# Taking the first four overflow tiles as one batch inside the last segment, and starting the next part's first pass later

## The chip, the cores and the metric

The kernel runs on one NeuronCore of a Trainium2 chip. The metric is the device time of one execution in microseconds (us). Before the change three runs gave 8543.35, 8543.91 and 8546.97 us, so the median is 8543.91 us. One further execution was profiled; its own time was 8539.33 us, and its trace spans 8537.6 us from the first to the last instruction.

Engines are called by their short names: PE (matrix products), DVE (vector), ACT (activation), POOL (GpSimd, which here issues every gather and scatter) and SP (which issues the plain transfers).

## The reference

640,000 edges connect 10,000 nodes. Every edge takes the 64 x 4 features of its source node, mixes the four components with a tensor that depends on the edge, scales the 64 channels with a learned radial weight, and adds the outcome to its destination node. A 64 x 64 product ends it.

```python
R = silu(edge_feat @ w_rad)                    # (E, 64)
xs = x[src]                                    # (E, 64, 4)
tp = einsum('eci,ef,ifo->eco', xs, Y, cg)      # (E, 64, 4)
agg = segment_sum((R[:, :, None] * tp).reshape(-1, 256), dst, N)
out = einsum('ncm,cd->ndm', agg.reshape(N, 64, 4), w_mix)
```

## The kernel before

**Sorting in two passes.** The edges are sorted by destination so that the sums can be matrix products. They are cut into three parts (30, 35.5 and 34.5 per cent; `SPLIT`). Pass 1 (`pass1`) routes the edges of one part into 18 groups of 576 nodes; pass 2 (`pass2`) routes the edges of one group into 18 buckets of 32 nodes. One group of one part is a *segment*. A pass first makes tables for some chunks (`digits`, `tables`: a chain of small steps that goes back and forth between PE, ACT and DVE), and then moves chunks of 12 tiles of 128 edges (`route`): DVE builds a spread payload X (line 578) and part of a one-hot matrix (594), ACT the rest of it (600, 601), PE multiplies them (608, 610), ACT evicts (615), and POOL scatters the rows to DRAM (619). In pass 2 a chunk continues the last row of the chunk before it, so PE needs the evicted chunk before (610).

**Messages.** `messages` takes the sorted buckets in units of 5 or 6 tiles: POOL gathers the source rows with one instruction per tile (line 915), DVE scales them (967), PE sums them over the edges of a bucket (980), DVE or ACT evicts the sums (1009, 1011), and in the last part PE mixes four buckets (1028), ACT evicts (1036) and SP writes the output rows (1037). The gather is five units ahead in the written order, and has seven buffers.

**Order of work.** `run` has three stages. First, pass 1 of part 0 alone. Then `groups`, in which PE, DVE and ACT keep the written order (a manual schedule) while SP and POOL are ordered by the framework. `groups` writes down one quarter step of a unit after another (`v`); before each it advances pass 1 of the next part until its share of the steps is done (`done < n * (v + 1 - at) / (end - at)`), and pass 2 of the next segment until it is paid off. At its beginning no bucket is ready yet: a loop runs pass 2 of the first segment (the small group of 7 buckets) until its payload is loaded, and takes one step of pass 1 of part 1 with each of its steps:

```python
while segs[0] not in self.pay:
    next(sort)
    if later:
        said = next(later[0][0])
        done += 0.0 if said == "held" else said or 1
```

**Overflow.** Rows of a group or a bucket that is full go to a list behind the table (`ovf`; counts in `kov`). The third stage handles these lists after everything else: `overflow_consts` builds two constants; `overflow` runs a hardware loop over the tiles of 128 rows of the first pass's list, and again over those of the second; `whole` redoes all edges if a table could not hold a case (a loop over zero or one). Each loop turn (`add`, line 1206) loads one tile, gathers its source rows (1210), finds rows with the same destination (1215 to 1228), reads the present output rows with a gather (1231), forms the messages (1246 to 1251), sums duplicates and mixes (1255, 1261), adds (1263) and scatters the rows back (1264). The loops' counts are read into registers (1154, 1181).

Of the kernel before, what the change touches and what calls it, by code (L numbers as in the profile page):

```python
# [40 lines left out]
FAR = 2097152.0  # L41
KR = 108
# [31 lines left out]
class Kernel:  # L74
    def __init__(self, ctx, tc, x, src, dst, Y, ef, w_rad, cg, w_mix, out):
# [45 lines left out]
        for q, tiles in ((self.p1, [z - a for a, z in self.part]), (self.p2, sum(self.gt, []))):  # L121
            q.none = -(-(q.ovf + sum((t + q.T - 1) // q.T for t in tiles) * P + 16) // q.stride) * q.stride
            q.rows = q.none
# [20 lines left out]
    def consts(self):  # L144
# [8 lines left out]
        self.zr = c.tile([16, max(self.p1.rw, self.p2.rw)], F, name="zr")  # L153
        nc.vector.memset(self.zr, 0.0)
        self.pid = iota("pid", [[0, 1]], cm=1)
        self.pid1 = iota("pid1", [[0, 1]], base=1, cm=1)
# [905 lines left out]
    def groups(self):  # L1062
# [12 lines left out]
        later, at = [], 0  # L1075
# [6 lines left out]
        while segs[0] not in self.pay:  # L1082
            next(sort)
            if later:
                said = next(later[0][0])
                done += 0.0 if said == "held" else said or 1
        acc = 0.0
        i = start = 0
        for v in range(4 * u):
# [13 lines left out]
            if i + 1 < len(segs):  # L1103
# [20 lines left out]
    def overflow_consts(self):  # L1124
        nc = self.nc

        m = self.ph.tile([P, 4], F, name="io", bufs=1)
        nc.gpsimd.iota(m, pattern=[[-1, 4]], base=P, channel_multiplier=1, allow_small_or_imprecise_dtypes=True)
        mi = self.ph.tile([P, 4], I32, name="ioi", bufs=1)
        nc.vector.tensor_copy(mi, m)  # L1130
        nc.vector.tensor_scalar(mi, mi, 3, None, op0=OP.bitwise_and)
        nc.vector.tensor_scalar(m, mi, 0.0, None, op0=OP.is_equal)
        self.wx = self.ph.tile([P, 2, 64, 4], F, name="wx")
        for h in range(2):
            nc.vector.tensor_tensor(self.wx[:, h], self.wm2[:, h, :].unsqueeze(2).to_broadcast([P, 64, 4]),
                                    m.unsqueeze(1).to_broadcast([P, 64, 4]), op=OP.mult)

        self.L = self.ph.tile([P, P], F, name="L")
        nc.vector.tensor_scalar(self.L, self.i128, self.pid, None, op0=OP.is_lt)

    def overflow(self, ps, count):

        nc, tc, wk, pm_ = self.nc, self.tc, self.ph, self.ps

        cp = pm_.tile([P, 512], F, name="cp", tag="misc", bufs=1)
        nc.tensor.matmul(cp[:16, 0:1], self.ones[0:1, :16], count, start=True, stop=True)
        zi = wk.tile([P, 1], I32, name="zi")
        nc.vector.scalar_tensor_tensor(zi[:16], cp[:16, 0:1], float(ps.ovf), self.pid[:16], op0=OP.add, op1=OP.add)
        nc.gpsimd.indirect_dma_start(
            out=ps.dst, out_offset=bass.IndirectOffsetOnAxis(ap=zi[:16, :], axis=0), in_=self.zr[:, :ps.rw],  # L1150
            in_offset=None, bounds_check=ps.rows - 1, oob_is_err=False)
        ni = wk.tile([1, 1], I32, name="ni")
        nc.vector.tensor_scalar(ni, count, ps.r / 128.0, 127.5 / 128 - 0.5, op0=OP.mult, op1=OP.add)
        n = nc.values_load(ni, min_val=0, max_val=(ps.rows - ps.ovf) * ps.r // P)
        flat = ps.dst.rearrange("r w -> (r w)")

        def load(k):
            pay = wk.tile([P, W], F, name="opay")
            nc.sync.dma_start(pay, flat[bass.ds(k * (P * W) + ps.ovf * ps.rw, P * W)].rearrange("(s w) -> s w", w=W))
            si = wk.tile([P, 1], I32, name="osi")  # L1160
            nc.vector.tensor_scalar(si, pay[:, 0:1].bitcast(I32), (1 << 14) - 1, None, op0=OP.bitwise_and)  # L1161

            dk = wk.tile([P, 1], I32, name="odk")
            nc.vector.tensor_scalar(dk, pay[:, 0:1].bitcast(I32), 14, None, op0=OP.logical_shift_right)  # L1164
            dst = wk.tile([P, 1], F, name="odst")
            nc.vector.tensor_scalar(dst, dk, 1.0 - TD, None, op0=OP.add)  # L1166
            return pay, si, dst

        with tc.For_i(0, n, 1) as k:  # L1169
            self.add(*load(k))  # L1170

    def whole(self):

        nc, wk = self.nc, self.ph
        m = wk.tile([64, 1], F, name="om")
        nc.vector.tensor_scalar(m, self.most, P + 0.5, None, op0=OP.is_ge)
        cp = self.ps.tile([P, 512], F, name="cw", tag="misc", bufs=1)
        nc.tensor.matmul(cp[0:1, 0:1], self.ones[:64, 0:1], m, start=True, stop=True)  # L1178
        ni = wk.tile([1, 1], I32, name="nw")
        nc.vector.tensor_scalar(ni, cp[0:1, 0:1], 1.0, None, op0=OP.min)  # L1180
        n = nc.values_load(ni, min_val=0, max_val=1)
        assert self.N % 125 == 0
# [3 lines left out]
        def load(k):  # L1186
            pay = wk.tile([P, W], F, name="opay")
            nc.vector.memset(pay, 0.0)
            si = wk.tile([P, 1], I32, name="osi")
            dk = wk.tile([P, 1], I32, name="odk")  # L1190
            t = bass.ds(k, 1)
            nc.sync.dma_start(si, self.src[:, t])
            nc.sync.dma_start(dk, self.dst[:, t])
            nc.sync.dma_start(pay[:, 1:5], self.Y[:, t, :].rearrange("p t f -> p (t f)"))
            nc.sync.dma_start(pay[:, 5:9], self.ef[:, t, :].rearrange("p t f -> p (t f)"))
            dst = wk.tile([P, 1], F, name="odst")
# [3 lines left out]
        with self.tc.For_i(0, n, 1):  # L1200
            nc.sync.dma_start(self.out.rearrange("(p b) f -> p b f", p=125),
                              zo.unsqueeze(1).to_broadcast([125, self.N // 125, 256]))
            with self.tc.For_i(0, self.NT, 1) as k:
                self.add(*load(k))

    def add(self, pay, si, dst):

        nc, wk, pm_ = self.nc, self.ph, self.ps
        xg = wk.tile([P, 64, 4], F, name="oxg")
        nc.gpsimd.indirect_dma_start(  # L1210
            out=xg.rearrange("p c i -> p (c i)"), out_offset=None, in_=self.x,
            in_offset=bass.IndirectOffsetOnAxis(ap=si, axis=0))

        pd = pm_.tile([P, 512], F, name="opd", tag="misc", bufs=1)
        nc.tensor.matmul(pd[:, :P], dst.to_broadcast([P, P]), self.ident, start=True, stop=True)
        eq = wk.tile([P, P], F, name="oeq")
        nc.vector.tensor_scalar(eq, pd[:, :P], dst, None, op0=OP.is_equal)

        dup = wk.tile([P, P], F, name="odup")
        nc.vector.tensor_tensor(dup, eq, self.L, op=OP.mult)  # L1220
        skip = wk.tile([P, 1], F, name="oskip")
        nc.vector.tensor_reduce(skip, dup, axis=AX.X, op=OP.max)
        em = wk.tile([P, 1], F, name="oem")
        nc.vector.tensor_scalar(em, dst, 0.5, None, op0=OP.is_lt)
        nc.vector.tensor_tensor(skip, skip, em, op=OP.max)
        di = wk.tile([P, 1], I32, name="odi")
        nc.vector.scalar_tensor_tensor(skip, skip, FAR, dst, op0=OP.mult, op1=OP.add)
        nc.vector.tensor_scalar(di, skip, -1.0, None, op0=OP.add)
        cur = wk.tile([P, 256], F, name="ocur")
        nc.vector.memset(cur, 0.0)  # L1230
        nc.gpsimd.indirect_dma_start(
            out=cur, out_offset=None, in_=self.out, in_offset=bass.IndirectOffsetOnAxis(ap=di, axis=0),
            bounds_check=self.N - 1, oob_is_err=False)

        pT = pm_.tile([P, 512], F, name="opT", tag="misc", bufs=1)
        nc.tensor.transpose(pT[:W, :P], pay, self.ident)
        sT = wk.tile([W, P], F, name="osT")
        nc.scalar.activation(sT, pT[:W, :P], AF.Copy)
        pr = pm_.tile([P, 512], F, name="opr", tag="misc", bufs=1)
        nc.tensor.matmul(pr[:, :80], sT, self.wo, start=True, stop=True)  # L1240
        R = wk.tile([P, 64], F, name="oR")
        nc.scalar.activation(R, pr[:, :64], AF.Silu)
        A = wk.tile([P, 16], F, name="oA")
        nc.scalar.activation(A, pr[:, 64:80], AF.Copy)
        V = wk.tile([P, 64, 4], F, name="oV")
        nc.vector.tensor_tensor(V, xg, R.unsqueeze(2).to_broadcast([P, 64, 4]), op=OP.mult)  # L1246
        M = wk.tile([P, 64, 4], F, name="oM")
        for o in range(4):
            nc.vector.tensor_scalar(M[:, :, o], V[:, :, 0], A[:, o:o + 1], None, op0=OP.mult)  # L1249
            for i in range(1, 4):  # L1250
# [83 lines left out]
```

## Time and profile before

| stage of the profiled execution | from, us | to, us |
|---|---|---|
| pass 1 of part 0, alone | 0 | about 512 |
| pass 2 of the first segment, with pass 1 of part 1 | 514.2 | 614.0 (first gather of a unit) |
| units, with pass 1 of the next part and pass 2 | 614.0 | 8466.8 (last plain output write has landed) |
| overflow lists: three tiles, all of the second pass | 8466.8 | 8537.6 |
| span / own time of this execution | | 8537.6 / 8539.33 |
| median of the three runs | | 8543.91 |

A row of the timeline gives the start, the duration, the engine, the line, the operation with its tiles and shapes, the count, and in brackets how long the engine had been idle and what ended that. A row of the windows gives, for a stretch, its length, each engine's busy time with the number of instructions, the granted TensorE clock (1.00 is full speed), the share of the DMA engines and their rate. A row of the grouped lines gives a line's count, its busy time and mean, and the idle time of the engine before it with what ended it.

### The profile page before, as it was taken

The numbers are of one execution on the slowest core, as the hardware profiler recorded it, in microseconds if no ns is written. First come the engines' busy times: TensorE is split into PE (matmuls) and PEld (weight loads), VectorE is DVE, ScalarE is ACT, GpSimd is POOL, SyncE is SP. The second block draws the span as 40 slices with busy tenths as digits, with TensorE's granted clock in tenths as the row PEclk, the third lists the DMA queues.
The fourth block names the chain that finished last, engine by engine and source line by source line (L and its number), as shares of the span: only waits on it lengthen the run. The fifth ranks groups of instructions, "written<-read, shape, count | busy, mean of one in ns | idle before, by whom it ended". The sixth has DMA issues, their size and how long they took to land. (4 is left out here: it accounts for less than half of the span.)

```text
span 8537.6 us, 148817 instructions
## 1 busy us (share of the span) xinstructions
PE 6849.6 (80%) x51885; PEld 6294.3 (74%) x51885; DVE 6833.0 (80%) x12901; ACT 4467.9 (52%) x12655; POOL 5984.1 (70%) x6255
## 2 busy tenths in 40 slices
PE   7977888888888788787787888876888878787875
PEld 6867777777778677777777777766777777677764
DVE  8988898889898789888888988876767767676743
ACT  6866666666566465555555655533433434343421
POOL 2236777677677767777777777777777777777774
PEclk9989999999899899899998998988888988898887
DMA  8313444344334434444444444444444444444442
GB/s 177 101 58 98 121 118 125 108 122 118 113 116 124 124 112 138 130 135 136 132 135 136 134 135 134 131 140 130 130 125 128 127 126 127 125 126 124 127 124 80
DMA packets 694591, 1056.58 MB, mean 124 GB/s; under 512 B 250979, under 2 KB 498340, under 8 KB 693840
## 3 DMA queue, kind: packets, MB, share of 16 engines
q0 software_dynamic: 284864, 746.68, 30.0%
q1 hardware_dynamic: 406384, 292.76, 12.3%
q8 instruction: 410, 6.72, 0.3%
q10 hardware_dynamic: 2592, 7.63, 0.3%
q14 instruction: 341, 2.79, 0.1%
HBM read 856.08 MB, written 203.45 MB: 124 GB/s over the span
## 5 line engine op out<-in xcount | busy, mean ns | idle before, releaser
L915 POOL DMA_INDIRECT xg<-in_x_dram,sidx x5321 | 5062.2, 951 | 1709.2 <-issue 1386.7
L608 PE MATMUL pr<-X,oh 128*128 128x135 f32 (+1 forms) x21112 | 2783.1, 291 | 400.2 <-ACT rt L615 256.8
L608 PEld LDWEIGHTS pr<-X,oh 128*128 128x128 f32 x21112 | 2662.8, 203 | 481.3 <-ACT rt L615 315.1
L980 PE MATMUL G<-S,xg 128*128 128x128 f32 x21284 | 2872.2, 296 | 155.5 <-DVE Gp L1009 116.7
L980 PEld LDWEIGHTS G<-S,xg 128*128 128x128 f32 x21284 | 2723.8, 210 | 198.7 <-DVE Gp L1009 142.9
L967 DVE TENSOR_TENSOR xg<-xg,pre 128x1536 f32<-128x1536 f32 (+1 forms) x939 | 1559.0, 1660 | 918.0 <-DMA xg<-in_x_dram,sidx 701.7
L600 ACT ACTIVATE sq<-i,rowf 128x128 f32<-128x128 f32 x6106 | 1876.1, 392 | 5.6 <-DVE rowf L565 2.4
L578 DVE TENSOR_TENSOR X<-dv,Wt 128x1512 f32<-128x1512 f32 (+3 forms) x905 | 1579.7, 1746 | 147.0 <-PE pr L608 100.0
L949 ACT ACTIVATE pre<-pre 128x384 f32<-128x384 f32 (+1 forms) x939 | 430.4, 458 | 1391.4 <-PE pre L946 1099.4
L601 ACT ACTIVATE oh<-sq,ones 128x896 f32<-128x896 f32 (+2 forms) x905 | 964.3, 1066 | 28.8 <-issue 1.4
L960 DVE TENSOR_TENSOR S<-dv,pay 128x768 f32<-128x768 f32 (+1 forms) x939 | 857.5, 913 | 64.3 <-PE G L980 20.1
L619 POOL DMA_INDIRECT grp<-rt,idx x417 | 418.6, 1004 | 573.8 <-ACT rt L615 244.9
L594 DVE TENSOR_TENSOR oh<-dv,rowf 128x640 f32<-128x640 f32 (+2 forms) x870 | 719.3, 831 | 0.5
L933 PE MATMUL pre<-identb,e 128*108 128x128 bf16 x1878 | 273.7, 229 | 500.6 <-DVE xg L967 492.9
L933 PEld LDWEIGHTS <-e 128*108 128x108 bf16 x1878 | 219.7, 132 | 572.1 <-issue 505.8
L619 POOL DMA_INDIRECT bkt<-rt,idx x488 | 488.6, 1001 | 192.5 <-issue 111.2
L938 ACT ACTIVATE sT<-pre 108x256 bf16<-108x256 f32 x939 | 351.5, 374 | 424.6 <-PE pre L933 423.2
L1028 PE MATMUL po<-wf,Gs 128*128 128x256 f32 (+2 forms) x1392 | 401.4, 453 | 160.0 <-DVE Gs L1009 158.8
L1028 PEld LDWEIGHTS po<-wf,Gs 128*128 128x128 f32 (+2 forms) x1392 | 289.8, 214 | 251.2 <-DVE Gs L1009 164.6
L896 ACT ACTIVATE e<-er 128x360 bf16<-128x360 f32 (+3 forms) x420 | 188.9, 450 | 416.1 <-DVE er L906 415.5
L615 ACT ACTIVATE rt<-pr 128x135 f32<-128x135 f32 (+1 forms) x905 | 242.5, 272 | 286.3 <-DMA bkt<-rt,idx 213.9
L548 ACT ACTIVATE pc<-pp 128x432 f32<-128x432 f32 (+4 forms) x453 | 233.5, 515 | 254.2 <-DVE pos L557 131.9
(247 smaller groups left out, 5257.3 us busy)
## 6 DMA issues: line engine op xcount, KB each, us to landing
xg<-in_x_dram,sidx POOLq DMA_INDIRECT x5321
sums<-Gp SPq DMA_DIRECT2D x626, 128.0 KB
old<-sums SPq DMA_DIRECT2D x626, 128.0 KB
bkt<-z SPq DMA_DIRECT2D x24, 994.5 KB
pay<-bkt SPq DMA_DIRECT2D x34, 486.0 KB
ys<-in_Y_dram SPq DMA_DIRECT2D x104, 96.0 KB
es<-in_edge_feat_dram SPq DMA_DIRECT2D x104, 96.0 KB
out_dram<-ot SPq DMA_DIRECT2D x69, 128.0 KB
```

What stands on the lines that cost most here:

```text
L578: nc.vector.tensor_tensor(X[:, :m, :].rearrange("p t (s w) -> p t s w", w=W), msk.unsqueeze(3).to_broadcast([P, m, ps.r, W]), QD[c // Q][1 ...
L594: nc.vector.tensor_tensor(oh[:, :v, :], self.v128.unsqueeze(1).to_broadcast([P, v, P]), row[:, o:o + v].unsqueeze(2).to_broadcast([P, v, P ...
L600: nc.scalar.activation(sq[:, u, :], self.i128, AF.Square, bias=to, scale=-1.0)
L601: nc.scalar.activation(oh[:, v:v + len(at), :], sq[:, :len(at), :], AF.Relu, bias=self.ones[:, 0:1], scale=-2.0)
L608: nc.tensor.matmul(pr[:, :ps.rw], oh[:, u, :], X[:, u, :], start=(u == 0), stop=(not on and u == m - 1))
L619: st = nc.gpsimd.indirect_dma_start(out=ps.dst, out_offset=bass.IndirectOffsetOnAxis(ap=idx[:, i:i + 1], axis=0), in_=RT.pop(c), in_offset ...
L915: nc.gpsimd.indirect_dma_start(out=xg[:, t, :], out_offset=None, in_=self.x, in_offset=bass.IndirectOffsetOnAxis(ap=si[:, u:u + 1], axis=0))
L933: nc.tensor.matmul(pre[:KR, 256 + 128 * h:384 + 128 * h], e[:, 36 * t:36 * t + KR], self.identb, start=True, stop=True)
L960: nc.vector.tensor_tensor(S[:, :ut], self.eq[:, :ut].unsqueeze(3).to_broadcast([P, ut, NB, 4]), pb[:, :, 1:5].unsqueeze(2).to_broadcast([P ...
L967: nc.vector.tensor_tensor(V, V, R.unsqueeze(3).to_broadcast([P, ut, 64, 4]), op=OP.mult)
L980: nc.tensor.matmul(G[:, h].rearrange("p n f -> p (n f)"), V[:, t, 32 * h:32 * h + 32, :].rearrange("p c i -> p (c i)"), S[:, t].rearrange( ...
L1028: nc.tensor.matmul(po[:nn, :256], Gs[:, h, f].rearrange("p b n -> p (b n)")[:, :nn], self.wf[:, h, f, :], start=(h + f == 0), stop=(h + f ...
```

## The change

Three things change.

1. The first four tiles (`LT = 4`) of the second pass's overflow list are handled in `batch`, whose steps are written between the quarter steps of the last segment, once that segment is sorted. It loads the four tiles with one transfer, gathers their source rows with four POOL instructions, compares all 512 destinations with each tile, and forms, sums and mixes the messages, with buffers that the sort no longer needs. Its reading and writing of the output rows (`put`) is written after the last unit. So that the four tiles can be read whatever their count is, `clear_buckets` zeroes the list's first 35 rows at the beginning.
2. What is left (the first pass's list, tiles beyond the fourth, `whole`) is put into one hardware loop over zero or one (`rest`), whose count `remains` has worked out in the last segment. Inside it, the loops take four tiles a turn.
3. The loop at the beginning of `groups` no longer takes steps of pass 1, and pass 1 of part 1 starts at quarter step 40 instead of 0.

```diff
-        later, at = [], 0
+        later, at = [], 40
...
         while segs[0] not in self.pay:
             next(sort)
-            if later:
-                said = next(later[0][0])
-                done += 0.0 if said == "held" else said or 1
+        batch, got = self.batch(), None
...
+            elif got is None:
+                if segs[-1] in self.pay:
+                    run(sort)
+                    self.remains()
+                    got = "begun"
+            elif got != "ready":
+                got = next(batch) or got
             next(main)
         assert not later
-        run(main)
-        run(sort)
+        for _ in main:
+            if got != "ready":
+                got = next(batch) or got
+        while got != "ready":
+            got = next(batch) or got
+        run(batch)
...
+    def clear_buckets(self):
+        a, m = self.p2.ovf, -(-LT * P // self.p2.r)
+        nc.sync.dma_start(self.p2.dst[a:a + m, :], self.z[:m, :self.p2.rw])
...
+    def join(self, al, pay, dst, di, xg, wx):
+        for t in range(OT):                      # 512 destinations against each tile
+            nc.tensor.matmul(pd[:, t * P:t * P + P], dst[:, t:t + 1].to_broadcast([P, P]), self.ident, ...)
+        for t in range(OT):
+            nc.vector.tensor_scalar(eq[t // 2][:, t % 2], pd, dst[:, t:t + 1], None, op0=OP.is_equal)
...
+        nc.vector.tensor_tensor(xg, xg, R..., op=OP.mult)        # 128 x 1024
+        for i in range(4):                       # four products and three sums of 128 x 1024
...
+        for h in range(2):                       # 32 matmuls 128 x 128, then 8 of 128 x 256
...
+    def put(self, al, di, xg):
+        nc.vector.memset(cur, 0.0)
+        for t in range(OT):
+            nc.gpsimd.indirect_dma_start(out=cur[:, t], in_=self.out, in_offset=...di[:, t:t + 1]...)
+        for t in range(OT):
+            nc.vector.tensor_tensor(cur[:, t], cur[:, t], xg[:, t]..., op=OP.add)
+            nc.gpsimd.indirect_dma_start(out=self.out, out_offset=...di[:, t:t + 1]..., in_=cur[:, t])
...
+    def rest(self):
+        with self.tc.For_i(0, self.nc.values_load(self.n[:, 3:4], min_val=0, max_val=1), 1):
+            self.wide(wx)
+            self.leftover(self.p1, self.kov[:, 0:1], self.n[:, 0:1], 0, wx)
+            self.leftover(self.p2, self.kov[:, 1:2], self.n[:, 1:2], LT * P, wx)
+            self.whole(self.n[:, 2:3], wx)
...
-            self.overflow_consts()
-            self.overflow(self.p1, self.kov[:, 0:1])
-            self.overflow(self.p2, self.kov[:, 1:2])
-            self.whole()
+            self.rest()
```

More of the change, by code (lines that the diff above doesn't have):

```diff
@@ L1163, in load @@
[L1163 to L1166, printed above, removed]
-            return pay, si, dst
-        with tc.For_i(0, n, 1) as k:
-            self.add(*load(k))
-    def whole(self):
-        nc, wk = self.nc, self.ph
[L1175 to L1182, printed above, removed]
+            pay = wk.tile([P, OT, W], F, name="opay")
```

280 lines of the change are left out of this document (187 added, 93 removed).

## The prediction

> **What bounds the kernel now.** I read the grouped lines first, then POOL's idle time over the first two parts, then the timelines of the places that the change touches: the beginning of the second stage, the last segment, the end. The page, and POOL's grouped lines between 1000 and 2800 us:
>
> ```profile
> span 8537.6 us, 148817 instructions
> L915 POOL DMA_INDIRECT xg<-in_x_dram,sidx x5321 | 5062.2, 951 | 1709.2 <-issue 1386.7
> ...
> L915 POOL DMA_INDIRECT xg<-in_x_dram,sidx x1142 | 1088.7, 953 | 391.0 <-issue 289.1 <-PE G L980 32.2 <-PE pre L946 8.8
> L619 POOL DMA_INDIRECT grp<-rt,idx x129 | 129.7, 1005 | 60.7 <-issue 25.0 <-ACT rt L615 7.9 <-ACT e L896 6.9
> L619 POOL DMA_INDIRECT bkt<-rt,idx x100 | 100.1, 1001 | 30.7 <-issue 21.9 <-ACT sq L600 1.5 <-ACT Gp L1011 1.2
> ```
>
> A gather takes 0.95 us and comes 0.30 us after the one before: 1.25 us each. In those 1800 us POOL has 1371 instructions: 1318.5 us busy and 1371 x 0.30 = 411 us between them; of 482.4 us idle only 71 (4 per cent) are real waits. So POOL's instruction count paces the units, and the other engines wait for it. Two stretches lie outside that: the beginning (no gather until 614 us) and the end.
>
> ```profile
> 514.00:614.00 100.00, 61.90 (x366) 51.42 (x366) 74.06 (x240) 49.73 (x150) 7.76 (x8) 0.69 0.11 31
> 520.00:540.00 20.00, 9.43 (x46) 6.05 (x47) 17.11 (x88) 2.11 (x11) 0.00 (x0) 0.50 0.07 23
> ...
> 8448.32 0.95 POOL L915 DMA_INDIRECT xg<-in_x_dram,sidx  x1 [0.30 <-issue]
> 8466.83 0.29 DVE L1139 TENSOR_SCALAR L<-i,pid 128x128 f32<-128x128 f32 x1 [6.33 <-DMA out_dram<-ot]
> 8467.17 0.13 DVE L1153 TENSOR_SCALAR ni<-kov 1x1 int32<-1x1 f32 x1
> 8472.42 0.20 PE L1146 MATMUL cp<-kov,ones 1*16 1x1 f32 x2 [7.42 <-ACTq L1154]
> 8480.13 1.03 POOL L1231 DMA_INDIRECT ocur<-out_dram,odi  x1 [1.72 <-DVE odi L1228]
> 8517.92 3.43 DMA oxg<-in_x_dram,osi
> 8530.33 1.03 POOL L1264 DMA_INDIRECT out_dram<-ocur,odi  x1 [8.68 <-DVE ocur L1263]
> 8533.72 0.19 PE L1178 MATMUL cw<-om,ones 64*1 64x1 f32 x2 [4.13 <-issue]
> 8533.94 0.14 DVE L1180 TENSOR_SCALAR nw<-cw 1x1 int32<-1x1 f32 x1 [3.90 <-PE cw L1178]
> ```
>
> The last plain output write has landed at 8466.8; all behind it, 8537.6 - 8466.8 = 70.8 us, is the overflow stage, a serial chain with everything else idle. Its list holds three tiles (the loop turned three times, for the second pass's list only), so `batch` takes all of them.
>
> **The end, part by part.** Removed: the 70.8 us. Added in the last segment: POOL's four gathers, 4 x 1.25 = 5.0 us, paid in full since POOL paces that segment; its queue has no wait there, and the indices are ready long before POOL, which lags the written order, comes to them. Also added there is the batch's work on PE, DVE and ACT:
>
> ```profile
> 8200.00:8270.00 70.00, 47.99 (x317) 43.52 (x316) 31.30 (x42) 11.07 (x28) 52.94 (x57) 0.85 0.49 140
> ...
> L967 DVE TENSOR_TENSOR xg<-xg,pre 128x1536 f32<-128x1536 f32 x9 | 15.8, 1755 | 36.2 <-DMA xg<-in_x_dram,sidx 36.2
> ...
> L980 PE MATMUL G<-S,xg 128*128 128x128 f32 x240 | 33.8, 305 | 0.6 <-DVE Gs L1009 0.5
> ...
> 8484.86 1.19 PE L1255 MATMUL opm<-oeq,oM 128*128 128x128 f32 x4 [4.71 <-DVE oM L1251]
> ```
>
> A PE row counts two records for one product of 128 columns. DVE: eight operations over 1024 columns at 1755 x 1024 / 1536 = 1.17 us are 9.4, some 8 for the comparisons and the small ones: 17 us, where DVE idles 70 - 31.3 = 38.7, nearly all of it (36.2) waiting for gathers. PE: 32 summing products, 12 short ones, 8 of double width, as 60 products: at the segment's 33.8 / 120 = 0.28 us 17 us, at the idle stage's 1.19 / 2 = 0.60 us 36 us, where PE idles 22. The steps take some 30 quarter steps, 7.5 units. POOL has seven buffers and may run about four units (30 us) ahead while PE is late, and some 20 units are left to catch up. So I cost it at nothing; without that cover it is at most 36 - 22 = 14 us. The batch's load stands in SP's queue behind fetches of old sums, and DVE's decoding of it is in the written order: behind it wait the products of one unit, 7.5 us at most, under the same cover. `remains` (some nine operations of 0.14 us and one product) is hidden likewise.
>
> Behind the last unit `put` stays. From the landing: four gathers of output rows at 1.03 + 0.30 = 1.3 us; the fourth starts 3.9 us on and lands 3.43 us later, at 7.3. Then four scatters. One takes 8533.72 - 8530.33 = 3.4 us until the next work can go on. Whether the four wait for one another the trace can't show: the loop ends between them. Chained they end at 7.3 + 13.6 = 20.9; unchained at 7.3 + 3.9 + 3.4 = 14.6. I take the chain: all four write one tensor, and `put` lacks the declaration of independence that the stores of line 619 have (lines 622 to 624). The jump over `rest`: nearest rows are the end of before (8537.6 - 8533.94 = 3.7) and the entry of the first, empty loop (8472.42 - 8467.17 = 5.2); nothing if it passes under the last scatter. I take 3.7. Sum: 70.8 - 20.9 - 3.7 - 5.0 = 41.2 us saved; between 70.8 - 20.9 - 5.2 - 5.0 = 39.7 and 70.8 - 14.6 - 5.0 = 51.2.
>
> The trace's one scatter decides 3.4 us a link. The Trainium skill, "DMA: Bandwidth & Descriptors" (section "Two DMAs through the same engine are not ordered"), says that only a completion semaphore orders dependent transfers, which speaks for the chain; its section "Anatomy of one DMA — SWDGE (gpsimd) path" gives about 2.0 us plus bytes / 436e3, for 131 KB an estimate of 2.3 us a link, with which the chain would be 9.2 and not 13.6 us. The measurement decides.
>
> **The beginning.** In the 100 us before the first gather the sort of the first segment (four chunks) shares the written order with pass 1 of part 1:
>
> ```profile
> 517.68 0.20 DVE L782 TENSOR_SCALAR dg<-Wt 128x40 int32<-128x40 int32 x1 [3.15 <-DMA Wt<-grp]
> 537.09 0.16 DVE L514 TENSOR_TENSOR idx<-rk,dest 128x4 int32<-128x4 f32 x1
> 546.47 1.84 DVE L578 TENSOR_TENSOR X<-dv,Wt 128x1620 f32<-128x1620 f32 x1
> 559.74 1.85 DVE L578 TENSOR_TENSOR X<-dv,Wt 128x1620 f32<-128x1620 f32 x1 [3.48 <-PE pr L608]
> ...
> 562.82 0.34 DVE L575 TENSOR_TENSOR dv<-dv,slot 128x168 f32<-128x168 f32 x1
> 563.28 1.73 DVE L578 TENSOR_TENSOR X<-dv,Wt 128x1512 f32<-128x1512 f32 x1
> ...
> 587.68 4.40 PE L608 MATMUL pr<-X,oh 128*128 128x126 f32 x24 [4.65 <-ACT rt L615]
> 592.12 0.72 DVE L578 TENSOR_TENSOR X<-dv,Wt 128x540 f32<-128x540 f32 x1 [0.35 <-PE pr L608]
> 592.49 2.95 PE L608 MATMUL pr<-X,oh 128*128 128x135 f32 x24
> 597.13 0.81 DVE L594 TENSOR_TENSOR oh<-dv,rowf 128x640 f32<-128x640 f32 x1
> 604.69 0.97 POOL L619 DMA_INDIRECT bkt<-rt,idx  x1 [2.47 <-ACT rt L615]
> 606.84 0.38 SPq L822 DMA_DIRECT2D pay<-bkt  x1
> 614.04 0.99 POOL L915 DMA_INDIRECT xg<-in_x_dram,sidx  x1 [8.38 <-DVE didx L869]
> ...
> L619 POOL DMA_INDIRECT grp<-rt,idx x4 | 3.9, 970 | 71.0 <-ACT rt L615 71.0
> ```
>
> The tables take 19.6 us (517.7 to 537.3), the way to the first X 9.2, four chunks a pitch of about 15 us (559.74 to 592.12 are two), the last X to the last store 12.6, store to payload load 2.2, load to first gather 7.2. Without pass 1 I take 16.5 for the tables (their steps stay serial), 6 to the first X, a pitch of 5 (PE's 4.40 at the low clock plus the carried row), 8 to the last store, and 5 more for the tables of the next segment, which run beside: 517.7 + 16.5 + 6 + 15 + 8 + 5 + 2.2 + 7.2 = 577.6. The first gather comes 36 us earlier. Bounds: nothing, if the chain only waits; 45 by the work, since pass 1's share of DVE's 74.06 us is about eight chunks of 0.34 + 1.73 + 0.81 + 0.3 = 3.2 (26 us) and one table chain (15), 41 in all, and waits go with it.
>
> The clock is 0.50 between 520 and 540 us and a chunk's 24 records take 4.40 us at one place and 2.95 at another. This agrees with the Trainium skill, "TensorE: Matmul & The Clock Gate" (section "HAM oscillation — how this bites in real kernels"), which warns of idle gaps of PE over about 3.4 us; it speaks against the change, as pass 1's products filled gaps. By full clock the ramp would be about 4 us shorter than I sum.
>
> What is moved must still be done: eight chunks and a table chain go into the units between quarter step 40 and the end of part 0. On POOL these are only the four stores that ran before 614 us, 4 x 1.27 = 5.1 us; the other engines' 41 us are hidden if POOL's pace hides them, and given back in full if not. POOL waits 4 per cent, so I take a value near the lower end, 15 us. The moved transfers of SP (destinations, sources, payload of the first blocks) stand behind writes of sums there, and DVE's decoding of them waits in the written order, once, inside these 15. Net gain 36 - 15 = 21 us; between 45 - 5 = 40 gained and 41 lost, if the ramp isn't shortened and all comes back.
>
> The constants moved to the start and the zeroing of 35 rows cost some 0.5 us.
>
> **Sum.** 41.2 + 21 - 0.5 = 61.7 us. The profiled execution's 8539.33 (1.7 above its span) becomes 8477.6; that execution was 4.6 us faster than the median of the runs shown, so against the median it is 8543.9 - 61.7 = 8482 us. 0.2 per cent, 17 us, is about what a measurement can tell from no change.
>
> **Rivals.**
> *The beginning gives nothing* (0.2): the 36 us come back from the other engines. For: DVE is busy three quarters of that stretch and more later. Against: POOL's 4 per cent. 8543.9 - 41.2 + 0.5 = 8503.
> *All bounds well* (0.12): scatters unchained, jump hidden, 40 at the beginning. 8543.9 - 51.2 - 40 = 8453.
> *The written order, not POOL, sets part 0* (0.04, slower): the table chain of pass 1, some 20 hand-offs between PE, ACT and DVE, now stops running units, at about 2 us each (40), with its 41 us of work, and the ramp is not shorter. It decides once this costs more than the end saves: 81 - 41 = 40 slower, 8584. Against: it needs 80 us more of POOL waits where 1800 us have 71.
> *The change does not do what it says* (0.04): the loops of `rest` still turn, through a fourth list or a fifth tile. Three entries of 5.2 us and one turn of about 25 undo the end's gain: 8523. Against: three tiles.
>
> The forecast has 0.6. The range reaches from the best case to the first rival with the last segment's cover gone (8503 + 14), rounded outwards: 8450 to 8518. It leaves out the last two. Faster by over 0.2 per cent: 0.6 + 0.2 + 0.12 = 0.92 (the last rival lies about on the line); within 0.04; slower 0.04.
>
> **What would show it.** Right: no loop turns behind the last plain write; four gathers 1.3 us apart, four scatters 3.4 us apart (1.3 if unchained), end some 25 us after the landing; four more POOL gathers in the last segment with no wait beyond 0.30; first unit gather near 578 us; POOL waits between 600 and 2800 us up by no more than about 15. Wrong: a first gather after 600, POOL waiting for PE in the last segment, or POOL's waits in part 0 up by 40.

## The result and the profile after

The changed kernel takes 8498.58 us in the median of six runs (8493.23 to 8501.77); the kernel before, on the same chip, takes 8546.07 us (8543.35 to 8549.97). The ratio is 0.9944, 95% interval 0.9931 to 0.9956: 47.5 us less. The prediction said 8482 us, so it forecast 61.7 us and got 47.5. The profiled execution of the changed kernel took 8493.53 us. In this document, "the lead" at the n-th gather (counted from 0) is how much earlier that gather of source rows for the units starts than in the kernel it is compared with.

First the span and the POOL rows between 1000 and 2800 us of the changed kernel (the line numbers have moved: 915 is now 926, 619 is 630, 980 is 991).

```profile
span 8491.8 us, 148473 instructions
...
L926 POOL DMA_INDIRECT xg<-in_x_dram,sidx x1120 | 1067.4, 953 | 406.4 <-issue 294.8 <-PE G L991 59.7 <-PE pre L957 10.1
L630 POOL DMA_INDIRECT grp<-rt,idx x129 | 129.5, 1004 | 62.9 <-issue 25.9 <-ACT rt L626 12.6 <-DVE rk L523 5.3
L630 POOL DMA_INDIRECT bkt<-rt,idx x100 | 100.3, 1003 | 34.1 <-issue 21.0 <-ACT rt L626 3.7 <-DVE dv L968 2.1
```

The gather still takes 0.95 us. Counted as in the prediction, POOL's real waits in these 1800 us are the idle 503.4 us less 1349 x 0.30, that is 98.7; they were 71. And there are 1120 gathers where there were 1142: the units run slower here.

The beginning, from the timeline of the changed kernel:

```profile
541.85 1.84 DVE L589 TENSOR_TENSOR X<-dv,Wt 128x1620 f32<-128x1620 f32 x1
...
545.47 1.84 DVE L589 TENSOR_TENSOR X<-dv,Wt 128x1620 f32<-128x1620 f32 x1
...
561.48 0.97 POOL L630 DMA_INDIRECT bkt<-rt,idx  x1 [0.80 <-ACT rt L626]
...
572.22 0.99 POOL L926 DMA_INDIRECT xg<-in_x_dram,sidx  x1 [9.77 <-DVE didx L880]
```

The first X stands at 541.9 us, the second 3.6 us behind it, the last store at 561.5, and the first unit gather at 572.2 where it was at 614.0.

The end, from the timeline of all engines:

```profile
8434.45 0.94 POOL L926 DMA_INDIRECT xg<-in_x_dram,sidx  x1 [0.30 <-issue]
...
8458.17 1.01 POOL L1242 DMA_INDIRECT ocur<-out_dram,osm  x1 [22.78 <-issue]
8459.49 1.00 POOL L1242 DMA_INDIRECT ocur<-out_dram,osm  x1 [0.31 <-issue]
...
8460.79 1.18 POOL L1242 DMA_INDIRECT ocur<-out_dram,osm  x1 [0.30 <-DMA ocur<-out_dram,osm]
...
8462.27 0.99 POOL L1242 DMA_INDIRECT ocur<-out_dram,osm  x1 [0.30 <-issue]
...
8465.80 1.03 POOL L1247 DMA_INDIRECT out_dram<-ocur,osm  x1 [2.53 <-DVEq L1378]
8469.35 1.00 POOL L1247 DMA_INDIRECT out_dram<-ocur,osm  x1 [2.53 <-issue]
8472.26 0.97 POOL L1247 DMA_INDIRECT out_dram<-ocur,osm  x1 [1.91 <-issue]
8475.23 0.97 POOL L1247 DMA_INDIRECT out_dram<-ocur,osm  x1 [1.99 <-issue]
```

No loop turns. Four gathers of output rows stand 1.3 to 1.5 us apart, four scatters 2.9 to 3.6 us apart. But the span ends at 8491.8, 16.6 us after the last scatter has started. What lies there are instructions of POOL's sequencer, which the timeline doesn't show; the instructions by line do (line, engine, instruction, count: duration in ns least/median/most, first and last start). In the changed kernel, the loop's line 1378 and the line of the program's end:

```profile
L1378 POOLq INC_SWDGE_SEM  x1: 1979/1979/1979, 8477.8 to 8477.8; - x1
...
L1444 POOLq DRAIN  x3: 40/103/7417, 8483.5 to 8491.5; - x3
```

And in the kernel before, the line of its first loop:

```profile
L1169 POOLq DRAIN  x4: 41/1269/7864, 8489.4 to 8515.3; - x4
L1169 POOLq INC_SWDGE_SEM  x3: 226/253/1786, 8469.0 to 8515.0; - x3
```

The last transfer is in at 8477.8; then POOL works 2.0 us on a semaphore step (INC_SWDGE_SEM) and, from 8483.5 on, 7.4 us on a DRAIN. The kernel before had the same pair, but around its first loop turn: the step of 1.8 us at 8469.0, ahead of that turn, and the DRAIN of 7.9 us at 8489.4, just behind its scatter. Later ones there took 0.23 to 0.25 us and 0.04 to 2.5 us.

The account of the two profiled executions, which differ by 45.8 us in span:

| stretch | before, us | after, us | difference |
|---|---|---|---|
| start to the first unit gather | 614.0 | 572.2 | -41.8 |
| first unit gather to the 5100th | 7553.7 | 7573.5 | +19.8 |
| 5100th to the last (the batch's place) | 280.6 | 288.8 | +8.2 |
| last unit gather to the first work behind the last plain write | 18.5 | 23.7 | +5.2 |
| from there to the end | 70.8 | 33.6 | -37.2 |

(In the kernel before the first work behind the last plain write is the row of 8466.83; in the changed one it is the gather of 8458.17.)

### The profile page after: what moved, and what is told of

It reads as the page before. It is cut to its first block, busy times and chain, and to the rows that moved or that the text cites. A ratio compares the mean times of both kernels' runs of the same rounds, so it can differ in the third digit from the quotient of the medians.

```text
span 8491.8 us, 148473 instructions
## 1 busy us (share of the span) xinstructions
PE 6828.0 (80%) x51942; PEld 6287.4 (74%) x51942; DVE 6828.5 (80%) x12848; ACT 4463.2 (53%) x12650; POOL 5986.1 (70%) x6256
## 5 line engine op out<-in xcount | busy, mean ns | idle before, releaser
L619 PE MATMUL pr<-X,oh 128*128 128x126 f32 (+1 forms) x21112 | 2775.1, 291 | 398.8 <-ACT rt L626 233.7
L612 ACT ACTIVATE oh<-sq,ones 128x896 f32<-128x896 f32 (+2 forms) x905 | 964.1, 1065 | 28.5 <-ACT sq L611 0.9
L971 DVE TENSOR_TENSOR S<-dv,pay 128x768 f32<-128x768 f32 (+1 forms) x939 | 857.5, 913 | 64.6 <-PE G L991 20.9
L605 DVE TENSOR_TENSOR oh<-dv,rowf 128x640 f32<-128x640 f32 (+1 forms) x870 | 720.1, 831 | 0.5
```

Source lines behind the costliest of these rows:

```text
L605: nc.vector.tensor_tensor(oh[:, :v, :], self.v128.unsqueeze(1).to_broadcast([P, v, P]), row[:, o:o + v].unsqueeze(2).to_broadcast([P, v, P ...
L612: nc.scalar.activation(oh[:, v:v + len(at), :], sq[:, :len(at), :], AF.Relu, bias=self.ones[:, 0:1], scale=-2.0)
L619: nc.tensor.matmul(pr[:, :ps.rw], oh[:, u, :], X[:, u, :], start=(u == 0), stop=(not on and u == m - 1))
L971: nc.vector.tensor_tensor(S[:, :ut], self.eq[:, :ut].unsqueeze(3).to_broadcast([P, ut, NB, 4]), pb[:, :, 1:5].unsqueeze(2).to_broadcast([P ...
```

## The experiments

In the session of the first four experiments every kernel, the one before included, took about 10.6 ms; their ratios are to the kernel before in that session, and the two that this concerns were run again later.

**The end alone, and the beginning alone.** For the end alone:

```diff
-        later, at = [], 40
+        later, at = [], 0
...
         while segs[0] not in self.pay:
             next(sort)
+            if later:
+                said = next(later[0][0])
+                done += 0.0 if said == "held" else said or 1
```

> The end of the change alone: the batch beside the last segment and the one loop behind it, with pass 1 of part 1 begun at the start as in the kernel before. Theory (the sizes read from the traces): the end's stage is 36 us shorter, four more gathers cost 5 us, so about 30 us faster than before (8516 us), the first unit gather near 614 us, the stage behind the last plain output write about 34.5 us. Rival 1 (the sum of the prediction holds for the end, and the beginning gives less than half of what was forecast): 41 us faster (8505 us). Rival 2 (the beginning gives nothing at all): 47 us faster (8499 us).

Measured: 10559.41 against 10591.88 us, ratio 0.9975 (0.9965 to 0.9985), 32 us less by the medians and 26 by the ratio, near the theory's 30.

The beginning alone makes the opposite edit to the kernel before (at = 40, no pass 1 in the loop).

> The beginning alone: the kernel before with pass 1 of part 1 begun at quarter step 40 of the units, its end untouched. Theory: the first unit gather is some 42 us earlier (near 572 us), some 23 us come back between the first and the last gather, net 18 us faster (8528 us). Rival 1 (the forecast's 15 us given back): 27 us faster (8519 us). Rival 2 (the beginning gives nothing, the work that is moved comes back in full): no change, 8546 us, the first gather earlier and the last one at the old place.

Measured: 10586.65 us, ratio 0.9999 (0.9988 to 1.0009). There the beginning gave nothing, as in rival 2. The POOL row of that run says why it is another case:

```profile
L915 POOL DMA_INDIRECT xg<-in_x_dram,sidx x5321 | 5071.9, 953 | 3270.4 <-issue 1413.2 <-PE G L980 828.4 <-remote 558.7
```

POOL's gathers have 3270 us of idle time ahead of them, 1857 of it real waits (1709 and 322 in the first profile): in that session POOL did not pace the units. The 20th gather had a lead of 47.0 us on the kernel with the end alone, the 80th 75.6, the 400th 28.5, the 1400th none: it was 9.6 us late. With POOL waiting for other engines, the moved work came back in full. Why that session was slower is not settled: the granted TensorE clock was 0.83 in it and 0.90 in the others, and its stage of units had waits on every engine that the kernel before doesn't show elsewhere. Both kernels were run again later, where the kernel before took 8553.4 us.

> The end alone, on a chip where the gathers pace the units again. Theory (from the times of the n-th gather in the kernels before and after): the end's stage gives 36 us, the last segment takes 8 us back (four gathers at 1.25 and 3 us more), so 28 us faster than before less what the last plain write happens to cost: 8516 to 8521 us; the n-th gather within 3 us of the kernel before up to the 5100th. Rival: the whole 47.5 us are the end's, 8499 us.

Measured: 8525.68 us, ratio 0.9969 (0.9957 to 0.9981), 27.7 us less.

> The beginning alone, on a chip where the gathers pace the units again. Theory: the 80th gather is 70 us earlier than before, 46 us of it come back by the 1400th, and 22 us stay to the end: 8524 us. Rival 1: all of it comes back, as on the chip where every kernel took 10.6 ms: 8546 us. Rival 2: the 15 us that the prediction gave back, with the 70 us that are really won: 8491 us.

Measured: 8532.49 us, ratio 0.9974 (0.9965 to 0.9983), 20.9 us less. 27.7 + 20.9 = 48.6, and the whole change gave 47.5: within the intervals, about 10 us each way, the two halves add up. The theory's split holds: about 28 us from the end, about 21 from the beginning.

**Where pass 1 begins.** Two kernels change only the start of pass 1 in the units:

```diff
-        later, at = [], 40
+        later, at = [], 0        # at0; 400 in at400
```

> The changed kernel with pass 1 of part 1 beginning at quarter step 0 of the units (not 40), still none of it beside the first sort. Theory (moved work costs the same wherever it stands in part 0, about two thirds of what it had cost at the beginning): the first gather stays at 572 us, the 80th is only some 45 to 50 us earlier than in the kernel before, the lead at the 1400th is 22 us as with 40; 8498 us, within 4 us. Rival (the units' first 40 quarter steps without pass 1 are what gives the 22 us): the lead falls to 0 to 10 us, 8508 to 8520 us.

> The changed kernel with pass 1 of part 1 beginning at quarter step 400, so that it is done in 728 quarter steps and not in 1088, half again as dense. Theory (the moved work is paid wherever it stands): the lead at the 400th gather is 100 us or more and falls to 15 to 25 us by the 1400th, 8498 us within 6 us. Rival 1 (GpSimd paces, and hides the work until a bound): the dense stretch passes that bound, the lead at the 1400th is negative, 8525 us or more. Rival 2 (the stretch without pass 1 hides more than the dense one costs): 8480 us.

Measured, in the session of the second runs: 8494.40 us with 0, ratio 0.9935 (0.9919 to 0.9950); 8597.54 us with 400, ratio 1.0052 (1.0036 to 1.0067). By the ratios the start at 0 can't be told from the changed kernel's 0.9944, and 8494.40 even lies in the 8498 within 4 us that its theory gave; the gathers tell more. The start of the n-th unit gather in the four kernels of that session, from their timelines (us; the first column has pass 1 as in the kernel before, the others give their lead on it, and the last row is the difference of two starts over 800):

| n | the end alone | the beginning alone (40) | at0 | at400 |
|---|---|---|---|---|
| 0 | 626.7 | 43.7 | 49.7 | 46.1 |
| 80 | 789.6 | 67.1 | 51.9 | 71.8 |
| 400 | 1283.9 | 50.0 | 41.0 | 125.1 |
| 600 | 1608.4 | 48.4 | 39.1 | 141.1 |
| 1400 | 2859.1 | 19.1 | 35.8 | -71.3 |
| 5100 | 8176.8 | 13.6 | 33.6 | -75.1 |
| us a gather, 600 to 1400 | 1.563 | 1.600 | 1.568 | 1.829 |

The theory of both expectations falls: the moved work isn't paid alike wherever it stands (at the 1400th gather the lead of at0 is 35.8 us where the theory said 22), and at400 ended 44 us slower than the kernel before, as its rival 1 said. The table shows a loan. Units without pass 1 beside them run at (1158.8 - 717.8) / 320 = 1.378 us a gather in at400 (80th to 400th), so a later start gains while it lasts. But pass 1 has to be done by quarter step 1128: from 0 it has 1128 quarter steps, from 40 it has 1088 (4 per cent denser), from 400 it has 728 (55 per cent denser). With 0 the units keep the old pace, 1.568 against 1.563. With 40 they lose 0.037 us a gather, 30 us in 800 gathers, and more than the loan of the first 40 quarter steps (67.1 - 51.9 = 15 us) is gone; with 400 they lose 0.266.

POOL's grouped rows between 1600 and 2850 us, in the changed kernel, with 0 and with 400:

```profile
L926 POOL DMA_INDIRECT xg<-in_x_dram,sidx x783 | 745.9, 953 | 280.9 <-issue 207.4 <-PE G L991 33.2 <-PE pre L957 8.5
L630 POOL DMA_INDIRECT grp<-rt,idx x87 | 87.4, 1004 | 40.2 <-issue 18.6 <-DVE rk L523 5.3 <-DVE oh L605 4.9
```

```profile
L926 POOL DMA_INDIRECT xg<-in_x_dram,sidx x800 | 762.3, 953 | 272.7 <-issue 207.5 <-PE G L991 22.6 <-PE pre L944 5.3
L630 POOL DMA_INDIRECT grp<-rt,idx x85 | 85.3, 1004 | 37.1 <-issue 15.8 <-ACT rt L626 7.5 <-ACT e L907 6.1
```

```profile
L926 POOL DMA_INDIRECT xg<-in_x_dram,sidx x678 | 647.1, 954 | 331.4 <-issue 169.9 <-PE G L991 98.8 <-PE stp L468 21.3
L630 POOL DMA_INDIRECT grp<-rt,idx x120 | 120.7, 1006 | 75.5 <-ACT rt L626 39.3 <-issue 19.5 <-DVE oh L605 4.5
```

Gathers per 1250 us fall from 800 to 783 to 678. More stores of pass 1 explain part of it (85, 87, 120 of them, 1.3 us each), waits for PE's products (PE G) more: 22.6, 33.2 and 98.8 us. So the cover of POOL's pace has no room left at the density of the kernel before, which is what the prediction's "POOL waits 4 per cent" hid. Which of the other engines sets that limit the rows don't settle: with 400, in the same 1250 us, DVE is busy 1106 us and PE 1053.

**The drain at the end.** One line, ahead of the batch's gathers of output rows, behind the last unit's gathers:

```diff
         while got != "ready":
             got = next(batch) or got
+        self.tc.keep_in_program_order(self.nc.gpsimd.drain())
         run(batch)
```

> The changed kernel with one more GpSimd drain, between the last unit's gathers and the four gathers of output rows, where GpSimd idles for 23 us. Theory: the 7.4 us of the drain at the very end are paid once for all the gathers and stores since the last drain; taken in the idle stretch they leave under 1.5 us for the drain at the end: 6 to 7 us faster than the changed kernel (8492 us). Rival 1 (the drain's 7.4 us belong to the four scatters ahead of it, or to the end of a program): the last drain still takes about 7.4 us and the time stays at 8498 us. Rival 2 (the early drain keeps GpSimd until after the batch is ready): the four gathers start later than before, no gain or a loss of up to 4 us.

Measured: 10552.00 us, ratio 0.9969 (0.9959 to 0.9979). That alone can't be told from the 0.9975 of the end without it. The trace can: the extra drain took 14.96 us, but it begins at 10444.4, beside the last gathers of the units, which end at 10452.5; 6.8 us of it lie behind them, in a stretch in which POOL waited 41.5 us for the plain writes anyway. The one at the end took 0.71 us instead of 7.42 and the semaphore step 0.34 instead of 1.98, and from the first gather of output rows to the end of the span are 10519.1 - 10494.0 = 25.1 us, where the changed kernel has 33.6. The theory's 6 to 7 us became 8.5: 6.7 of the drain, as it said, and 1.6 of the semaphore step, which it didn't name.

Is it the first drain that is dear, or what has piled up since the last one? The same line ahead of the second stage:

```diff
+        self.tc.keep_in_program_order(self.nc.gpsimd.drain())
         while segs[0] not in self.pay:
             next(sort)
```

> The changed kernel with one more GpSimd drain just ahead of the second stage (behind some 130 of the 6240 GpSimd transfers), where GpSimd is idle for over 50 us. It tells a first-time cost from a backlog. Theory 1 (the drain pays for the transfers issued since the last one): the early drain is short or as long as its transfers take to land, the one at the end still takes 7.4 us and the semaphore step ahead of it 2.0 us; the time is that of the changed kernel. Theory 2 (what costs is the first drain of a program): the last drain takes under 1 us, the step ahead of it about 0.3 us, 8 us faster than the changed kernel.

Measured: 8501.28 us in the one run (the kernel before 8551.32). The early drain, the semaphore step and the drains at the end:

```profile
L1093 POOLq DRAIN  x1: 3353/3353/3353, 518.2 to 518.2; - x1
...
L1379 POOLq INC_SWDGE_SEM  x1: 1619/1619/1619, 8487.4 to 8487.4; - x1
...
L1445 POOLq DRAIN  x3: 46/103/5937, 8492.7 to 8499.2; - x3
```

An early drain leaves 5.9 of the 7.4 us and 1.6 of the 2.0 us at the end. So neither theory holds in full, but most of the cost is not that of a first drain; it goes with what POOL has done since the last one (about 6100 transfers here, eight in drain_idle). It doesn't go with the time: the last drain took 7.417 us in the kernel with the end alone in the session of 10.6 ms and in that of 8.5 ms. Nor is it in plain proportion to the transfers: only 123 of 6238 stand ahead of the early drain here, and a fifth of the cost is gone. How it grows between 8 and 6100 was not tried.

**Four scatters without a chain.** `put` lacks the declaration that the passes' stores have:

```diff
-            nc.gpsimd.indirect_dma_start(
+            st = nc.gpsimd.indirect_dma_start(
                 out=self.out, out_offset=bass.IndirectOffsetOnAxis(ap=di[:, t:t + 1], axis=0), in_=cur[:, t], in_offset=None,
                 bounds_check=self.N - 1, oob_is_err=False)
+            if t:
+                self.tc.declare_no_dep(st.ins, group=key, reason="the rows of a batch are apart")
+            self.tc.add_to_no_dep_group(key, st.ins)
```

> The changed kernel with the four scatters of the batch declared independent of one another, as the stores of the passes are. Theory: the four scatters were chained at 3.0 to 3.5 us a link; without the chain they follow each other by their issue of 1.3 us, 5 to 6 us faster (8493 us). Rival 1 (the transfers themselves queue behind one another): the starts are 1.3 us apart, and the last one lands no earlier, 8498 us. Rival 2: the drain at the end takes up what the chain gave, growing from 7.4 us to 12 or more.

Measured: 10553.89 us, ratio 0.9967 (0.9956 to 0.9978). From the first gather of output rows to the end 10544.7 - 10516.5 = 28.2 us instead of 33.6: 5.4 less, as the theory said. The last drain stayed at 7.42 us, so rival 2 falls, and rival 1 with it.

**Both, and then with the start at 0.**

> The changed kernel with both: the extra GpSimd drain in the idle stretch behind the last gathers, and the four scatters declared independent. Theory: the two gains lie behind one another on the chain of the end, so they add up: 8 us from the drain (with the shorter semaphore step ahead of it) and 5 to 6 us from the scatters, the stage behind the last plain output write shrinks from 34.5 to about 21 us, the whole 61 us faster than the kernel before where the changed kernel was 47.5 us faster. Rival: without the chain the last drain finds transfers still under way, and takes back 3 us or more.

Measured: 8479.17 us (8478.45 to 8482.64) against 8545.97, ratio 0.9923 (0.9909 to 0.9937), 66.8 us less. The end of it, from the timeline, and then its drains (1137 is the extra one) and its semaphore step by line:

```profile
8434.84 0.94 POOL L926 DMA_INDIRECT xg<-in_x_dram,sidx  x1 [0.30 <-issue]
8457.43 1.01 POOL L1245 DMA_INDIRECT ocur<-out_dram,osm  x1 [21.64 <-DMA out_dram<-ot]
...
8465.14 1.03 POOL L1250 DMA_INDIRECT out_dram<-ocur,osm  x1 [2.59 <-DVEq L1384]
8466.47 1.00 POOL L1250 DMA_INDIRECT out_dram<-ocur,osm  x1 [0.30 <-issue]
8467.78 0.97 POOL L1250 DMA_INDIRECT out_dram<-ocur,osm  x1 [0.30 <-POOLq L1384]
8469.05 0.97 POOL L1250 DMA_INDIRECT out_dram<-ocur,osm  x1 [0.30 <-issue]
```

```profile
L1137 POOLq DRAIN  x1: 14155/14155/14155, 8428.4 to 8428.4; - x1
...
L1384 POOLq INC_SWDGE_SEM  x1: 339/339/339, 8471.6 to 8471.6; - x1
...
L1450 POOLq DRAIN  x3: 46/103/710, 8475.8 to 8477.0; - x3
```

The scatters are 1.3 us apart. From 8457.4 to the end (8477.3) are 19.9 us, 13.7 less than in the changed kernel; the two gains apart were 8.5 + 5.4 = 13.9, so they add up. (The theory's 61 us in all lie within the interval of the ratio, 54 to 78 us.) The extra drain hides: POOL would have waited for the last plain write until 8457 in any case.

> The version with the early drain and the independent scatters, and with pass 1 of part 1 beginning at quarter step 0. Theory (from the times of the n-th gather: a start at 40 compresses pass 1 into 4 per cent fewer quarter steps, and each hundred gathers of part 0 takes 2.7 us longer): some 12 us faster than the same version with 40, about 8468 us where the kernel before takes 8546. Rival (the lead that 0 showed was that of one chip): the two are within 3 us.

> The same version with pass 1 of part 1 beginning at quarter step 40, on the same chip as its twin with 0. Theory: 66 us faster than the kernel before, as in its first run, and 12 us slower than the twin; units of part 0 between the 600th and the 1400th gather at 1.595 us a gather against 1.567. Rival: no difference from the twin.

Measured, on one chip: 8473.37 us with 0 (8465.93 to 8478.13), ratio 0.9911 (0.9896 to 0.9926), and 8485.17 us with 40 (8483.09 to 8491.94), ratio 0.9929 (0.9915 to 0.9942). The kernel before took 8551.32. The start at 0 is 11.8 us faster where the theory said 12; each kernel's runs spread over some 10 us, so that the two agree so closely is chance, but no run with 0 is as slow as any with 40. The units' pace between the 600th and the 1400th gather is 1.567 and 1.599 us, as the theory said. The version with the drain, the free scatters and the start at 0 is 78 us faster than the kernel before, where the changed kernel was 47.5 us faster.

## Why the prediction was right, and by which terms it missed

The direction, the mechanism of each part and the range (8450 to 8518) were right; 8482 was 16.6 us too low. 2.2 of these are the kernel before itself (8546.07 and not 8543.91); the rest lies in the terms of the sum, which are taken here from the two profiled executions (45.8 us apart, where the medians are 47.5 apart).

- **"The jump over `rest`: 3.7 us" (0 to 5.2).** This is the term that failed: from the landing of the last scatter to the end the trace has 8491.8 - 8477.8 = 14.0 us. 3.7 was read at the end of the kernel before, where POOL's drain took 0.29 us, behind loop turns that had drained already. The long drain stood in that trace too, 7.9 us in the first loop turn, among the sequencer's instructions, which the timeline leaves out; with the loop gone it is paid at the end. drain_idle shows that it can be moved back into idle time. With the drain paid, 10519.1 - 10513.5 = 5.6 us are left for the jump and the end, just above the upper bound.
- **The chain of `put`: 20.9 us.** Right as a mechanism and nearly in size. From the first gather to the last landing it took 19.6 us (8458.2 to 8477.8); unchained it gave 5.4 us where the prediction's two sums differ by 6.3. The estimate of 2.3 us a link that the prediction formed from the Trainium skill, "DMA: Bandwidth & Descriptors" (section "Anatomy of one DMA — SWDGE (gpsimd) path"), is not borne out: the links took 2.9 to 3.6 us. About 1.0 us of each is POOL's own instruction, and the wait behind it, 1.9 to 2.5 us, is of the estimate's size.
- **"Four gathers x 1.25 = 5.0" and the batch's work at nothing.** The four gathers stand 1.25 us apart with no wait beyond 0.30, as said. But the stretch cost 8.2 us, and as much in the kernel with the end alone. The cover by POOL's buffers held; the sum priced DVE's products against DVE's own idle time only, and left out that four gathers of the units beside them take longer, 3.2 us together (last section).
- **The last write.** The stretch from the last gather to the work behind the last plain write grew by 5.2 us, which the sum had at nothing. 2.9 of them are the second last mix of PE, 6.66 us in this execution at a granted clock of 0.55 against 3.72 before at 1.00. In the other profiles it is 5.3 to 5.4 us (the clock 0.68 in those of best and of the beginning alone, which has no batch) or, in the session of 10.6 ms, 3.72; so these 2.9 us go with the clock of the execution and not with the batch. The other 2.3 us, between the end of the last mix and the first gather of output rows, come back in every kernel with the batch, and their cause was not looked for.
- **"36 earlier, 15 given back, net 21".** The net is right (22.0 at the 5100th gather; 20.9 for the beginning alone), but by luck, since the parts are not. The first gather came 41.8 us earlier: the first X was right (540.2 forecast, 541.9 found), the pitch was 3.6 us and not 5, and from the last store to the gather it took 10.7 us where 14.4 were forecast, 5 of them for the next segment's tables. Then the lead grew to 70.0 us at the 80th gather, since the first 40 quarter steps carry no pass 1, and fell to 24.7 at the 1400th. The prediction named the moved work as what would come back; the runs put the density of pass 1 in its place. At a start of 0 that density stays and 16 us come back (49.7 to 33.6), near the 15 forecast; a start at 40 adds a loan that costs more than it brings.

As the sum: 61.7 forecast, less 9.0 at the end (33.6 against 20.9 + 3.7), less 3.2 in the last segment, less 5.2 at the last write, plus 1.0 at the beginning (41.8 - 19.8 against 21) and 0.5 for the constants, which the trace doesn't show apart, gives 45.8, the difference of the two spans.

The signs named: POOL waits between 600 and 2800 us "up by no more than about 15" was a poor test. Over that stretch they went down, since the kernel before has 14 us of its beginning in it; between 1000 and 2800 us they went up by 28, between the two marks. "POOL waiting for PE in the last segment" did not happen: from 8080 us to the last gather no instruction of POOL waits longer than 0.32 us.

The rivals: "The beginning gives nothing" was wrong where POOL paces the units (20.9 us) and right in the session in which POOL did not pace the units, by the condition that the prediction named. "All bounds well" had two parts in reach, but only once written: unchained scatters and a drain in idle time are worth 13.7 us together. "The written order sets part 0" came nowhere near its 40 us slower with a start at 40. With a start at 400 the kernel was 44 us slower, but whether by the written order or by the load of PE and DVE the rows don't tell.

## What to carry to other kernels

When a stage at the end is removed, look at what its first loop turn had paid once, sequencer instructions included, for it will be paid at the new end; an idle stretch of the same engine just before is the place for it. Work that is put off until later is a loan: what counts is how dense it becomes in the time that is left, so a small later start can cost more than it gains. And scatters to rows that are apart have to be declared so, or they go one by one.

## What the runs showed of the hardware that was not expected

**A drain of POOL is not free.** After some 6200 transfers it took 7.4 to 7.9 us, after eight 0.7 us, and the semaphore step ahead of it 1.8 to 2.0 against 0.34 us. The Trainium skill, "VectorE: DVE Perf Modes" (section "The DRAIN you can't avoid"), gives about 12 ns for the drains that the runtime adds ahead of and behind a program, on all five engines. Whether the drains of these traces are of that kind isn't shown; at the end of the changed kernel the other engines' took 7 to 17 ns, which agrees, and POOL's first took 7417 ns, which doesn't.

**Some of POOL's gathers take longer beside the batch's DVE work.** POOL's timeline of the changed kernel where the batch is worked off, and DVE's beside it:

```profile
8209.83 0.95 POOL L1162 DMA_INDIRECT oxg<-in_x_dram,osm  x1 [0.30 <-issue]
...
8213.58 0.95 POOL L1162 DMA_INDIRECT oxg<-in_x_dram,osm  x1 [0.30 <-issue]
...
8217.33 1.68 POOL L926 DMA_INDIRECT xg<-in_x_dram,sidx  x1 [0.30 <-issue]
...
8220.57 1.77 POOL L926 DMA_INDIRECT xg<-in_x_dram,sidx  x1 [0.30 <-issue]
...
8225.13 2.00 POOL L926 DMA_INDIRECT xg<-in_x_dram,sidx  x1 [0.30 <-issue]
...
8228.68 1.57 POOL L926 DMA_INDIRECT xg<-in_x_dram,sidx  x1 [0.30 <-issue]
8230.56 0.96 POOL L926 DMA_INDIRECT xg<-in_x_dram,sidx  x1 [0.30 <-issue]
```

```profile
8216.97 1.23 DVE L1204 TENSOR_TENSOR oxg<-oxg,oR 128x1024 f32<-128x1024 f32 x1 [19.96 <-DMA oxg<-in_x_dram,osm]
...
8220.30 1.22 DVE L1209 TENSOR_TENSOR oM<-oxg,oA 128x1024 f32<-128x1024 f32 x1
8221.43 1.22 DVE L1209 TENSOR_TENSOR oN<-oxg,oA 128x1024 f32<-128x1024 f32 x1
...
8225.10 1.22 DVE L1209 TENSOR_TENSOR oN<-oxg,oA 128x1024 f32<-128x1024 f32 x1
...
8228.22 1.22 DVE L1213 TENSOR_TENSOR oM<-oM,oN 128x1024 f32<-128x1024 f32 x1
8229.48 1.23 DVE L1209 TENSOR_TENSOR oN<-oxg,oA 128x1024 f32<-128x1024 f32 x1
8230.74 1.22 DVE L1213 TENSOR_TENSOR oM<-oM,oN 128x1024 f32<-128x1024 f32 x1
```

Four gathers take 1.68, 1.77, 2.00 and 1.57 us and not 0.95, together 3.2 us more, just while DVE forms the batch's products of 1024 columns from two operands. It belongs to the batch, not to one execution: in the kernel with the end alone four gathers at the same place take 1.79, 1.77, 1.99 and 1.57 us, and the one with the beginning alone has none above 1.42. The longest of each (the last of the three figures, in ns) by their lines:

```profile
L926 POOL DMA_INDIRECT xg<-in_x_dram,sidx x5321: 942/946/1991, 626.7 to 8465.6; - x198
```

```profile
L915 POOL DMA_INDIRECT xg<-in_x_dram,sidx x5321: 941/946/1412, 583.0 to 8443.8; - x198
```

The Trainium skill, "GPSIMD Engine Reference" (section "Specifications"), says that GpSimd shares its access to SBUF with VectorE and that the two contend when VectorE reads two inputs there. The rows go with that. Each of the four begins within an operation whose two inputs both lie in SBUF (lines 1204, 1209, 1213) and ends 0.81 to 0.82 us behind the end of it; the gather of 8230.56 begins 0.15 us before such an end and takes 0.96. The kernel's own large DVE operations (lines 589, 605, 971, 978) have one input in PSUM, where PE's products also go: 2384 gathers of this execution begin within one of them, and none takes more than 1.04 us. Of 53 that begin within an operation with both inputs in SBUF (the four, and short ones of lines 388, 455, 456 and 463 in the sort's tables), 49 take more than 1.0. Batch products with one input in PSUM were not tried.
